# An FFT and GeGLU kernel on one core: value products from two separate matmul passes, sums on DVE, products on POOL, and another split of the PSUM banks

## The chip, the cores and the metric

The kernel runs on one core of one Trainium2 chip. The metric is the device time of one execution in microseconds (us). The engines are PE (TensorE matmuls; its weight loads are listed apart as PEld), DVE (VectorE), ACT (ScalarE), POOL (GpSimd) and SP, whose queue issues nearly all the stores.

## The reference

```python
x = np.fft.fft(np.fft.fft(x, axis=1), axis=2).real        # x: 8 x 3008 x 256
x = x.reshape(24064, 256)
g   = x @ w_gate                                          # 256 -> 1536
val = x @ w_val
out = (0.5 * g * (1 + erf(g / sqrt(2))) * val) @ w_out    # 1536 -> 256
```

## The kernel before

For each of 8 batches the kernel makes the transform with matmuls (stages A, Z and then E and O), and then the feed-forward part. The symmetry of a real input's transform is used: the values of a pair of mirrored tokens are E + O and E - O. A batch is cut into three chunks of 512, 512 and 481 columns, and the 1536 features into 12 blocks of 128, so there are 24 x 12 = 288 blocks. For the gate and for the value, a block accumulates E and O in a PSUM bank, the result for the first token of each pair is read, and then a third matmul with the weights M = -2 x O turns the same bank into the mirrored token's result. That makes six matmuls a block.

```python
def l1_first(ci, fc):                     # per block: E + O
    pg, pv = ps_g(), ps_v()
    for nm, ps in (("g", pg), ("v", pv)):
        nc.tensor.matmul(ps[:, :n], W[nm, "E"][:, fs], EO[:, 0, ...], start=True, stop=False)
        nc.tensor.matmul(ps[:, :n], W[nm, "O"][:, fs], EO[:, 1, ...], start=False, stop=True)
    gl = gelu_tile()
    nc.scalar.activation(gl[:, :n], pg[:, :n], AF.Gelu)
    nc.vector.tensor_tensor(st["h"][:, fc, 0, :n], gl[:, :n], pv[:, :n], op=ALU.mult)

def l1_second(ci, fc):                    # one block later: the mirrored tokens
    for nm, ps in (("g", pg), ("v", pv)):
        nc.tensor.matmul(ps[:, :n], W[nm, "M"][:, fs], EO[:, 1, ...], start=False, stop=True, ...)
    ...                                   # gelu on ACT, product on DVE, written in reverse order
# l2_unit: 12 matmuls h x w_out into ps_o, evicted by ACT, stored from SP
# PSUM, eight banks: gate g 2, value v 2, output o 2, transforms dft 2
```

The transform of the next batch is woven into the blocks of the present one as filler, and a scheduler fixes the order of the instructions on each engine when the kernel is built.

## Time and profile before

The median is 757.7 us (756.9 to 758.0). The first three lines of the profile's page give the span, and for each engine the busy time, its share of the span and the number of instructions:

```profile
span 755.9 us, 14118 instructions
## 1 busy us (share of the span) xinstructions
PE 732.6 (97%) x5328; PEld 478.6 (63%) x5328; DVE 491.7 (65%) x826; ACT 441.4 (58%) x829; POOL 24.2 (3%) x57
...
```

The view by windows shows a stretch of the steady state: its length, then the busy time of PE, PEld, DVE, ACT and POOL with their instruction counts, the clock, and the DMA share and GB/s:

```profile
...
core 0: us, PE busy (x) PEld busy (x) DVE busy (x) ACT busy (x) POOL busy (x), PEclk, DMA share, GB/s
...
350.00:450.00 100.00, 99.70 (x736) 66.04 (x735) 65.67 (x109) 58.89 (x110) 1.02 (x2) 1.00 0.23 50
...
```

In the view of groups (line, engine, operation, tiles, shapes, count, then total busy us, the mean ns of one, and the engine's idle time before them with what ended it), these are the groups that the change touches, and the output matmuls:

```profile
...
L519 PE MATMUL ps_o<-Wo_sb,h_sb 128*128 128x256 bf16 x2112 | 273.1, 272 | 0.5 <-DVE out_sb L530 0.5
...
L484 DVE TENSOR_TENSOR h_sb<-gelu_sb,ps_v 128x512 bf16<-128x512 bf16 x192 | 131.9, 687 | 122.5 <-ACT gelu_sb L483 74.2 <-PE ps_v L481 28.9 <-PE ps_g L496 7.7
L502 DVE TENSOR_TENSOR h_sb<-gelu_sb,ps_v 128x512 bf16<-128x512 bf16 x192 | 130.8, 682 | 28.7 <-ACT gelu_sb L500 27.3
...
L496 PE MATMUL ps_g<-EO_sb,WgM 128*128 128x512 bf16 x192 | 72.9, 380 | 1.1 <-ACT gelu_sb L483 0.7
...
```

The view of waits, for PE alone (us in total, how often, the longest):

```profile
...
PE ps_g L349 <- DVE x_sb L227: 10.6, 4, 5.5
PE ps_o L349 <- DVE x_sb L227: 3.2, 2, 2.3
PE ps_g L496 <- ACT gelu_sb L483: 0.7, 1, 0.7
...
```

PE is busy 99.7 of 100 us, has no idle time worth naming outside the first microseconds, and is the only engine near its limit. A 512-column matmul is recorded as 0.380 us, but consecutive ones start 0.215 us apart. This is the timeline (start, duration in us, engine, what) of a stretch in the middle:

```profile
...
308.02 0.69 DVE L484 TENSOR_TENSOR h_sb<-gelu_sb,ps_v 128x512 bf16<-128x512 bf16 x1 [1.17 <-ACT gelu_sb L483]
308.13 0.38 PE L496 MATMUL ps_v<-EO_sb,WvM 128*128 128x512 bf16 x1
...
308.34 0.38 PE L496 MATMUL ps_g<-EO_sb,WgM 128*128 128x512 bf16 x1
...
308.62 1.01 DVE L365 CAST A_sb<-ps_dft 128x384 bf16<-128x384 f32 x2
308.76 0.38 PE L496 MATMUL ps_v<-EO_sb,WvM 128*128 128x512 bf16 x1
...
```

Between 308.34 and 308.76 PE stood still for 0.2 us, and began again just after the DVE product that reads a value bank (308.02 to 308.71) had ended. No view counts this as idle, because the record of the earlier matmul lasts until 308.72. The Trainium skill says why one must expect it (Perfetto Trace Analysis, section "Tensor Engine Instruction"): the end of a matmul in the profile is estimated from its size, not observed.

### The profile page before, as it was taken

The numbers are of one execution on the slowest core, as the hardware profiler recorded it, in microseconds if no ns is written. First come the engines' busy times: TensorE is split into PE (matmuls) and PEld (weight loads), VectorE is DVE, ScalarE is ACT, GpSimd is POOL, SyncE is SP. The second block draws the span as 40 slices with busy tenths as digits, with TensorE's granted clock in tenths as the row PEclk, the third lists the DMA queues.
The fourth block names the chain that finished last, engine by engine and source line by source line (L and its number), as shares of the span: only waits on it lengthen the run. The fifth ranks groups of instructions, "written<-read, shape, count | busy, mean of one in ns | idle before, by whom it ended". The sixth has DMA issues, their size and how long they took to land.

```text
span 755.9 us, 14118 instructions
## 1 busy us (share of the span) xinstructions
PE 732.6 (97%) x5328; PEld 478.6 (63%) x5328; DVE 491.7 (65%) x826; ACT 441.4 (58%) x829; POOL 24.2 (3%) x57
## 2 busy tenths in 40 slices
PE   2999999999999999999999999999999999999997
PEld 2545666666666666666666666666666666666566
DVE  7688667666676666766667665676666766655552
ACT  5666565556655656556655565656565565655551
POOL 7200000000000000000000000000000000000000
PEclk9999999999999999999999999999999999999999
DMA  9941511421115111151112411111111111111113
GB/s 240 214 86 25 114 29 43 87 64 30 43 32 118 32 39 36 36 111 39 39 34 43 107 39 33 43 29 39 30 43 31 38 29 43 33 39 39 43 40 69
DMA packets 36228, 43.42 MB, mean 57 GB/s; under 512 B 6620, under 2 KB 33244, under 8 KB 34652
## 3 DMA queue, kind: packets, MB, share of 16 engines
q1 hardware_dynamic: 32432, 30.47, 17.0%
q0 software_dynamic: 3136, 11.57, 8.1%
q8 instruction: 41, 0.67, 0.4%
q10 hardware_dynamic: 592, 0.49, 0.3%
q14 instruction: 27, 0.22, 0.1%
HBM read 29.43 MB, written 24.64 MB: 72 GB/s over the span
## 4 chain that ended last, share of the span: by engine, by line
PE 96%; DVE 2%; ACT 1%; issue 1%; DMA 1%; ACTq 0%
PE ps_o L519 33%; PE ps_g L480 9%; PE ps_v L480 9%; PE ps_v L496 9%; PE ps_g L496 8%; PE ps_g L481 8%; PE ps_v L481 8%; PE ps_dft L386 5%; PE ps_dft L349 3%; PE ps_dft L424 1%; PE ps_dft L411 1%; DVE x_sb L227 1%; DMA x_plain<-in_x_dram 1%; ACT gelu_sb L483 0%; PE ps_g L317 0%
## 5 line engine op out<-in xcount | busy, mean ns | idle before, releaser
L484 DVE TENSOR_TENSOR h_sb<-gelu_sb,ps_v 128x512 bf16<-128x512 bf16 (+1 forms) x288 | 195.1, 678 | 193.3 <-ACT gelu_sb L483 116.6
L519 PE MATMUL ps_o<-Wo_sb,h_sb 128*128 128x256 bf16 (+1 forms) x2304 | 298.6, 272 | 0.5 <-DVE out_sb L530 0.5
L519 PEld LDWEIGHTS <-h_sb 128*128 128x128 bf16 (+1 forms) x2304 | 227.2, 100 | 80.1 <-issue 8.6
L483 ACT ACTIVATE gelu_sb<-ps_g 128x512 bf16<-128x512 f32 (+1 forms) x288 | 169.5, 589 | 155.3 <-PE ps_g L481 153.5
L502 DVE TENSOR_TENSOR h_sb<-gelu_sb,ps_v 128x512 bf16<-128x512 bf16 (+1 forms) x288 | 193.2, 671 | 46.6 <-ACT gelu_sb L500 45.2
L500 ACT ACTIVATE gelu_sb<-ps_g 128x512 bf16<-128x512 f32 (+1 forms) x288 | 169.2, 588 | 36.1 <-PE ps_g L496 34.8
L496 PE MATMUL ps_g<-EO_sb,WgM 128*128 128x512 bf16 (+1 forms) x288 | 108.2, 376 | 1.1 <-ACT gelu_sb L483 0.7
L480 PE MATMUL ps_g<-EO_sb,WgE 128*128 128x512 bf16 (+1 forms) x288 | 107.8, 374 | 0.9
L496 PE MATMUL ps_v<-EO_sb,WvM 128*128 128x512 bf16 (+1 forms) x288 | 108.0, 375 | 0.7
L480 PE MATMUL ps_v<-EO_sb,WvE 128*128 128x512 bf16 (+1 forms) x288 | 107.8, 374 | 0.7
L481 PE MATMUL ps_g<-EO_sb,WgO 128*128 128x512 bf16 (+1 forms) x288 | 108.1, 375 | 0.0
L481 PE MATMUL ps_v<-EO_sb,WvO 128*128 128x512 bf16 (+1 forms) x288 | 108.0, 375 | 0.0
L537 ACT ACTIVATE out_sb<-ps_o 128x512 f32<-128x512 f32 x92 | 54.9, 597 | 77.0 <-PE ps_o L519 77.0
L386 PE MATMUL ps_dft<-CS,A_sb 128*128 128x256 bf16 x368 | 57.3, 274 | 0.0
L386 PEld LDWEIGHTS <-A_sb 128*128 128x128 bf16 x384 | 38.3, 100 | 25.7 <-issue 1.5
L349 PEld LDWEIGHTS <-x_sb 94*128 94x128 bf16 x512 | 32.0, 102 | 32.7 <-DVE x_sb L227 14.9
L481 PEld LDWEIGHTS <-WvO 128*128 128x128 bf16 x288 | 28.0, 97 | 31.3 <-issue 8.8
L396 DVE CAST Z_sb<-ps_dft 128x512 bf16<-128x512 f32 x66 | 45.1, 685 | 2.2 <-PE ps_dft L386 2.2
L480 PEld LDWEIGHTS <-WvE 128*128 128x128 bf16 x288 | 28.1, 98 | 26.1 <-issue 1.3
L365 DVE CAST A_sb<-ps_dft 128x384 bf16<-128x384 f32 x84 | 44.5, 551 | 0.1
L481 PEld LDWEIGHTS <-WgO 128*128 128x128 bf16 x288 | 28.0, 97 | 19.1 <-issue 13.2
L496 PEld LDWEIGHTS <-WvM 128*128 128x128 bf16 x288 | 28.1, 98 | 14.8 <-issue 0.7
(96 smaller groups left out, 319.8 us busy)
## 6 DMA issues: line engine op xcount, KB each, us to landing
out_dram<-out_sb SPq DMA_DIRECT2D x361, 64.0 KB, 2.0
x_sb<-in_x_dram POOLq DMA_DIRECT2D x14, 752.0 KB, 10.1
x_plain<-in_x_dram SPq DMA_DIRECT2D x4, 384.0 KB, 7.9
x_plain<-in_x_dram SPq DMA_DIRECT2D x2, 768.0 KB, 8.0
Wo_sb<-in_moe_w_out_dram POOLq DMA_DIRECT2D x2, 384.0 KB, 6.3
wg_hi<-in_moe_w_gate_dram SPq DMA_DIRECT2D x2, 256.0 KB, 3.7
wv_hi<-in_moe_w_val_dram SPq DMA_DIRECT2D x2, 256.0 KB
wg_lo<-in_moe_w_gate_dram SPq DMA_DIRECT2D x2, 256.0 KB, 4.4
```

The source lines that it names most:

```text
L349: nc.tensor.matmul(ps[:, jj * 96 : (jj + 1) * 96], xt[:, j0 + jj, cc * 128 : (cc + 1) * 128], G[:, j0 + jj, :], start=True, stop=True,)
L386: nc.tensor.matmul(ps[:, d * C : (d + 1) * C], A[:, cc, k2 + d, :], CS[:, cc, :], start=(cc == 0), stop=(cc == 1),)
L396: nc.vector.tensor_copy(_sub(Z, [[1, 2 * C]], k2 * C), ps)
L480: nc.tensor.matmul(ps[:, :n], W[nm, "E"][:, fs], EO[:, 0, c0 : c0 + n], start=True, stop=False)
L481: nc.tensor.matmul(ps[:, :n], W[nm, "O"][:, fs], EO[:, 1, c0 : c0 + n], start=False, stop=True)
L483: nc.scalar.activation(gl[:, :n], pg[:, :n], AF.Gelu)
L484: nc.vector.tensor_tensor(st["h"][:, fc, 0, :n], gl[:, :n], pv[:, :n], op=ALU.mult)
L496: nc.tensor.matmul(ps[:, :n], W[nm, "M"][:, fs], EO[:, 1, c0 : c0 + n], start=False, stop=True, skip_group_check=True)
L500: nc.scalar.activation(gl[:, :n], pg[:, :n], AF.Gelu)
L502: nc.vector.tensor_tensor(_sub(st["h"], [[-1, n]], (fc * 2 + 1) * TOK + n - 1), gl[:, :n], pv[:, :n], op=ALU.mult)
L519: nc.tensor.matmul(pso[:m, sign, :], st["h"][:, fc, sign, h0 : h0 + m], Wo_sb[:, fc, :], start=(fc == 0), stop=(fc == NFC - 1),)
L537: nc.scalar.activation(osb[:m], pso[:m], AF.Copy)
```

## The change

PE streams fewer columns. In two blocks in three the value is not accumulated: one matmul leaves E in a value bank, one leaves -2 x O in another, and DVE forms both sums. That drops one of the six matmuls. For this, channel 128, which sits in row 0 of O and which M leaves out, must be added to E by other means: PE broadcasts it once per chunk to all partitions (weights read with stride 0), and DVE adds it times a column of weights. POOL then makes one product for both tokens. To make room, the value gets three banks and the output one; the first transform packs rotate through seven banks instead of eight; the A casts go to ACT, and all later Z casts to DVE. The SBUF tiles for the output get three buffers instead of four, and a gelu tile now holds both tokens.

```diff
+    def apart(ci, fc):
+        return fc % 3 != 2 and (b, ci) != (0, 0)
 # l1_first, in such a block:
+        mm(pv, n, "v", "E", fs, E, True, True)
+        po = ps_v()
+        mm(po, n, "v", "M", fs, O, True, True)
+        nc.vector.scalar_tensor_tensor(ve[:, :n], EB_bufs[b][:, c0 : c0 + n], w128[:, fc : fc + 1],
+                                       pv[:, :n], op0=ALU.mult, op1=ALU.add)
+        nc.vector.scalar_tensor_tensor(vv[:, 0, :n], po[:, :n], -0.5, ve[:, :n], ...)
+        nc.vector.scalar_tensor_tensor(_sub(vv, [[-1, n]], TOK + n - 1), po[:, :n], 0.5, ve[:, :n], ...)
 # l1_second, in such a block: no value matmul, no DVE product
+        nc.gpsimd.tensor_tensor(st["h"][:, fc, :, :n], gl[:, :, :n], pv[:, :, :n], op=ALU.mult)
 # banks
-        ... tag="v", bufs=2 ...      tag="o", bufs=2
+        ... tag="v", bufs=3 ...      tag="o", bufs=1
-            tag = ("dft", "g", "v", "o")[turn[0] % 4]
+            tag, n = (("dft", 2), ("g", 2), ("v", 3))[turn[0] % 3]
 # the O pack: 128 columns (O and channel 128) become 64 + 64
+                    nc.tensor.matmul(ps[:, off : off + n], _sub(st["Z"], [[0, 128]], k2 * C + 128),
+                                     TPI[:, 0:n], start=True, stop=True)      # then cast to EB by ACT
 # evictions
-                s1_ev(j0, "VA" if j0 % 8 == 4 else "VV")
+                s1_ev(j0, "AA")
-                if (k2 // 2) % (2 if b == 0 else 4) == 1:     # Z cast on ACT, else DVE
+                if b == 0 and k2 // 2 % 2 == 1:
 # ... tiles, loads of w128, scratch tiles: cut
```

More of the change, by code (lines that the diff above doesn't have):

```diff
@@ L106, in h_tile, with EB_tile, ve_tile, v_tile @@
         return work_pool.tile([128, NFC, 2, TOK], BF16, tag="h", bufs=2, name="h_sb")
+    def EB_tile():
+        return work_pool.tile([128, HALF], BF16, tag="EB", bufs=2, name="EB_sb")
     def gelu_tile():
-        return work_pool.tile([128, TOK], BF16, tag="gelu", bufs=4, name="gelu_sb")
+        return work_pool.tile([128, 2, TOK], BF16, tag="gelu", bufs=4, name="gelu_sb")
+    def ve_tile():
+        return work_pool.tile([128, TOK], FP32, tag="ve", bufs=2, name="ve_sb")
+    def v_tile():
+        return work_pool.tile([128, 2, TOK], FP32, tag="v", bufs=2, name="v_sb")
     def osb_tile():
-        return work_pool.tile([128, 2, C], FP32, tag="osb", bufs=4, name="out_sb")
+        return work_pool.tile([128, 2, C], FP32, tag="osb", bufs=3, name="out_sb")
     def ps_g():
@@ L117, in ps_v @@
     def ps_v():
-        return psum_pool.tile([128, 512], FP32, tag="v", bufs=2, name="ps_v")
+        return psum_pool.tile([128, 512], FP32, tag="v", bufs=3, name="ps_v")
     def ps_o():
-        return psum_pool.tile([128, 2, C], FP32, tag="o", bufs=2, name="ps_o")
+        return psum_pool.tile([128, 2, C], FP32, tag="o", bufs=1, name="ps_o")
     def ps_dft():
@@ L164 @@
     rd = work_pool.tile([128, 2 * NPH], FP32, tag="Z", bufs=1, name="rd")
-    fp = const_pool.tile([128, C], FP32)
-    rp = const_pool.tile([128, C], FP32)
-    dc = const_pool.tile([128, C], FP32)
+    small = work_pool.tile([128, 4, C], FP32, tag="v", bufs=2, name="small")
+    fp, rp, dc, off = (small[:, i, :] for i in range(4))
     dt_ = const_pool.tile([128, 2 * K1], FP32)
-    off = const_pool.tile([128, C], FP32)
     col_m = const_pool.tile([128, 1], FP32)
@@ L176 @@
     dump = const_pool.tile([1, 1], FP32)
+    w128 = const_pool.tile([128, NFC], FP32)
     w_lo, w_hi = {}, {}
@@ L301, in load_w, with load_w128 @@
                         in_=ap_replace(w, ap=[[F, 128], [1, n]], offset=w.offset + r0 * F + f0))
+    def load_w128():
+        nc.gpsimd.dma_start(
+            out=w128[:, :],
+            in_=ap_replace(moe_w_val, ap=[[1, 128], [128, NFC]], offset=moe_w_val.offset + 128 * F))
     def load_wo():
@@ L325 @@
     EO_bufs = [None] * B
+    EB_bufs = [None] * B
     turn = [0]
@@ L332, in ps_any @@
             turn[0] += 1
-            tag = ("dft", "g", "v", "o")[turn[0] % 4]
-            return psum_pool.tile([128, 512], FP32, tag=tag, bufs=2, name=f"ps_{tag}")
+            tag, n = (("dft", 2), ("g", 2), ("v", 3))[turn[0] % 3]
+            return psum_pool.tile([128, 512], FP32, tag=tag, bufs=n, name=f"ps_{tag}")
         return ps_dft()
@@ L415, in e_pack, with b_pack, run, o_pack @@
             return run
-        def o_pack(gi, half):
+        def b_pack(gi):
+            def run():
+                if "EB" not in st:
+                    st["EB"] = EB_tile()
+                    EB_bufs[b] = st["EB"]
+                ps = st["ps_b"] = ps_dft()
+                for off, k2, n in cols[gi]:
+                    nc.tensor.matmul(
+                        ps[:, off : off + n], _sub(st["Z"], [[0, 128]], k2 * C + 128), TPI[:, 0:n],
+                        start=True, stop=True)
+                n = chunk_len[gi]
+                nc.scalar.activation(_sub(st["EB"], [[1, n]], chunk_off[gi]), ps[:, :n], AF.Copy)
+            return run
+        def o_pack(gi):
             def run():
@@ L420, in run @@
                 ps = ps_dft()
-                part = [c for c in cols[gi] if c[0] // 256 == half]
-                base = half * 256
-                for off, k2, n in part:
+                for off, k2, n in cols[gi]:
                     nc.tensor.matmul(
-                        _sub(ps, [[256, 2], [1, n]], off - base),
-                        st["Z"][:, k2, 128:256], _sub(TPI, [[K1, 2], [1, n]], 0), start=True, stop=True)
-                n = min(256, chunk_len[gi] - base)
-                off = HALF + chunk_off[gi] + base
-                nc.vector.tensor_copy(_sub(EO, [[1, n]], off), ps[:, 256 : 256 + n])
+                        ps[:, off : off + n], st["Z"][:, k2, 128:256], TPI[:, K1 : K1 + n], start=True, stop=True)
+                n = chunk_len[gi]
+                off = HALF + chunk_off[gi]
+                nc.vector.tensor_copy(_sub(EO, [[1, n]], off), ps[:, :n])
                 nc.scalar.activation(
-                    _sub(EO, [[1, n]], off, part_num=1), _sub(ps, [[1, n]], 0, part_num=1), AF.Copy)
+                    _sub(EO, [[1, n]], off, part_num=1), _sub(st["ps_b"], [[1, n]], 0, part_num=1), AF.Copy)
             return run
@@ L439, in dft_work @@
             work.append(e_pack(gi))
-            work.append(o_pack(gi, 0))
-            work.append(o_pack(gi, 1))
+            work.append(b_pack(gi))
+            work.append(o_pack(gi))
         return (work, s1_mm, s1_ev) if b == 0 else work
@@ L466, in ffn_work, with mm @@
         cstate = {}
+        def apart(ci, fc):
+            return fc % 3 != 2 and (b, ci) != (0, 0)
+        def mm(ps, n, nm, part, fs, src, start, stop, **kw):
+            nc.tensor.matmul(ps[:, :n], W[nm, part][:, fs], src, start=start, stop=stop, **kw)
         def l1_first(ci, fc):
             def run():
-                EO = EO_bufs[b]
                 n = chunk_len[ci]
                 c0 = chunk_off[ci]
+                E, O = (EO_bufs[b][:, i, c0 : c0 + n] for i in range(2))
                 if ci not in cstate:
@@ L476, in run @@
                 fs = slice(fc * 128, (fc + 1) * 128)
-                pg, pv = ps_g(), ps_v()
-                st["ps"][fc] = (pg, pv)
-                for nm, ps in (("g", pg), ("v", pv)):
-                    nc.tensor.matmul(ps[:, :n], W[nm, "E"][:, fs], EO[:, 0, c0 : c0 + n], start=True, stop=False)
-                    nc.tensor.matmul(ps[:, :n], W[nm, "O"][:, fs], EO[:, 1, c0 : c0 + n], start=False, stop=True)
-                gl = gelu_tile()
-                nc.scalar.activation(gl[:, :n], pg[:, :n], AF.Gelu)
-                nc.vector.tensor_tensor(st["h"][:, fc, 0, :n], gl[:, :n], pv[:, :n], op=ALU.mult)
+                pg = ps_g()
+                mm(pg, n, "g", "E", fs, E, True, False)
+                mm(pg, n, "g", "O", fs, O, False, True)
+                gl = gelu_tile()
+                nc.scalar.activation(gl[:, 0, :n], pg[:, :n], AF.Gelu)
+                pv = ps_v()
+                if apart(ci, fc):
+                    mm(pv, n, "v", "E", fs, E, True, True)
+                    po = ps_v()
+                    mm(po, n, "v", "M", fs, O, True, True)
+                    ve = ve_tile()
+                    nc.vector.scalar_tensor_tensor(
+                        ve[:, :n], EB_bufs[b][:, c0 : c0 + n], w128[:, fc : fc + 1], pv[:, :n],
+                        op0=ALU.mult, op1=ALU.add)
+                    vv = v_tile()
+                    nc.vector.scalar_tensor_tensor(
+                        vv[:, 0, :n], po[:, :n], -0.5, ve[:, :n], op0=ALU.mult, op1=ALU.add)
+                    nc.vector.scalar_tensor_tensor(
+                        _sub(vv, [[-1, n]], TOK + n - 1), po[:, :n], 0.5, ve[:, :n], op0=ALU.mult, op1=ALU.add)
+                    st["ps"][fc] = (pg, vv, gl)
+                else:
+                    mm(pv, n, "v", "E", fs, E, True, False)
+                    mm(pv, n, "v", "O", fs, O, False, True)
+                    nc.vector.tensor_tensor(st["h"][:, fc, 0, :n], gl[:, 0, :n], pv[:, :n], op=ALU.mult)
+                    st["ps"][fc] = (pg, pv, gl)
             return run
@@ L488, in run @@
             def run():
-                EO = EO_bufs[b]
                 n = chunk_len[ci]
                 c0 = chunk_off[ci]
+                O = EO_bufs[b][:, 1, c0 : c0 + n]
                 st = cstate[ci]
                 fs = slice(fc * 128, (fc + 1) * 128)
-                pg, pv = st["ps"].pop(fc)
-                for nm, ps in (("g", pg), ("v", pv)):
-                    nc.tensor.matmul(
-                        ps[:, :n], W[nm, "M"][:, fs], EO[:, 1, c0 : c0 + n],
-                        start=False, stop=True, skip_group_check=True)
-                gl = gelu_tile()
-                nc.scalar.activation(gl[:, :n], pg[:, :n], AF.Gelu)
-                nc.vector.tensor_tensor(
-                    _sub(st["h"], [[-1, n]], (fc * 2 + 1) * TOK + n - 1), gl[:, :n], pv[:, :n], op=ALU.mult)
+                pg, pv, gl = st["ps"].pop(fc)
+                mm(pg, n, "g", "M", fs, O, False, True, skip_group_check=True)
+                if apart(ci, fc):
+                    nc.scalar.activation(_sub(gl, [[-1, n]], TOK + n - 1), pg[:, :n], AF.Gelu)
+                    nc.gpsimd.tensor_tensor(st["h"][:, fc, :, :n], gl[:, :, :n], pv[:, :, :n], op=ALU.mult)
+                else:
+                    mm(pv, n, "v", "M", fs, O, False, True, skip_group_check=True)
+                    nc.scalar.activation(gl[:, 1, :n], pg[:, :n], AF.Gelu)
+                    nc.vector.tensor_tensor(
+                        _sub(st["h"], [[-1, n]], (fc * 2 + 1) * TOK + n - 1),
+                        gl[:, 1, :n], pv[:, :n], op=ALU.mult)
             return run
@@ L601 @@
         nc.gpsimd.tensor_copy(dump, w_hi["v"][0:1, F - 1 : F])
+        load_w128()
         load_wo()
```

## The prediction

> **What bounds it now.** TensorE. The page has PE busy 732.6 of 755.9 us (97%), the chain that ended last is 96% PE, and in every 100 us stretch from 150 to 650 us PE is busy 99.7 us, while DVE is busy 65 to 66 and ACT 59 to 60. PE's own waits add up to under 17 us, nearly all in the head. Granted clock 1.00. POOL is busy 24 us. One batch takes about 89 us.
>
> **Removed from PE.** A block (128 features x one chunk) has six matmuls of 512 or 481 columns; two blocks in three drop one. In the timeline consecutive 512-column matmuls start 0.215 us apart, so 481 columns cost about 0.203. The first chunk is left out: 15 chunks x 8 x 0.215 + 8 x 8 x 0.203 = 39 us. All of it is on the critical path.
>
> **Added to PE.** The O matmul of 128 columns becomes two of 64, one with channel 128 broadcast as weights: the same columns, 192 more weight loads. The eight 64-column matmuls of the E pack take about 0.24 us in the timeline, 30 ns each, so splitting costs a few ns apiece: 1 to 3 us in all, if a stride-0 weight load is as fast as a dense one. PE floor: 757.7 - 39 + 2 = 721 us.
>
> **DVE** (per batch with DFT work, now 58 us). Two products (0.687, 0.682 us) become three scalar_tensor_tensor in 24 of 36 blocks; that operation took 0.74 to 0.75 us at 128x512 in the weight fold, so I take 0.71 to 0.74: 24 x 2.15 = 51 us, plus 24 products 16, 12 Z casts 8, 3 O casts 2: 78 us. The 12 A casts go to ACT. PE will need about 84 us. By phase it is tighter: where Z and EO are made DVE needs about 2.28 us a block and PE 2.31; where A is made ACT needs 2.16 (two gelus 1.18, A 0.78, output 0.20) and PE 2.26. Both helpers become nearly full, coupled to PE through three value banks and two gate banks.
>
> **POOL.** 184 products of 1024 elements. The trace has 0.61 to 0.94 us for 256 elements; the Trainium skill (GPSIMD Engine Reference, section 3.1) measures 4497 ns for 2048, so 2.1 to 2.4 us by estimate, 4.7 us in the 7 us of three blocks: busy about 430 us, off the critical path. The skill (SBUF, Who interferes with whom) says a DVE instruction with one SBUF input does not contend with POOL; all the new ones have one SBUF and one PSUM tensor. The trace of before can't show this.
>
> **Sum.** Floor 721 plus stalls of some 2% (PE waiting for a value bank that DVE still reads, or for ps_dft and ps_g behind ACT): 735 us.
>
> **What would show it.** PE matmuls down 184 of 512/481 columns and up 192 of 64; PE busy about 715 and 96 to 98% of the span; DVE 600 to 630 us (83%); ACT 480 to 500; POOL 400 to 470. New PE waits: ps_v on the DVE sums, 5 to 20 us in total.
>
> **What would make it wrong.** POOL locking DVE out after all (products over 3 us, or DVE sums over 0.9): then about 760 or more. DVE sums at 0.69 and no stalls: 722. Broadcast weight loads at 100 ns each: +10 us. An instruction order fixed by a schedule that thinks DVE or POOL faster than it is: stalls in every block, 745 to 755.
>
> Chances: faster by over 2% 0.73, within 2% 0.23, slower 0.04. Range 722 to 750.

## The result, and the profile after

The changed kernel took 719.1 us (718.6 to 719.7), a ratio of 0.949 with a 95% interval of 0.948 to 0.951. A ratio here is the mean time of one kernel's fast runs over that of the other's of the same rounds, so it is not quite the ratio of the medians quoted. The direction was as predicted, but the time lies below the stated range (722 to 750): the gain is 38.6 us, where 22.7 were forecast. The same views as before:

```profile
span 716.7 us, 14298 instructions
## 1 busy us (share of the span) xinstructions
PE 688.0 (96%) x5274; PEld 460.5 (64%) x5336; DVE 572.3 (80%) x923; ACT 466.9 (65%) x892; POOL 412.2 (58%) x242
...
```

```profile
...
core 0: us, PE busy (x) PEld busy (x) DVE busy (x) ACT busy (x) POOL busy (x), PEclk, DMA share, GB/s
...
350.00:450.00 100.00, 99.16 (x774) 67.12 (x781) 82.26 (x133) 65.66 (x127) 60.31 (x31) 1.00 0.25 54
...
```

```profile
...
L551 POOL TENSOR_TENSOR h_sb<-gelu_sb,v_sb 128x1024 bf16<-128x1024 bf16 x120 | 257.2, 2144 | 190.2 <-ACT gelu_sb L550 104.0 <-DVE v_sb L530 46.7 <-ACT gelu_sb L517 31.0
...
L524 DVE SCALAR_TENSOR_TENSOR ve_sb<-EB_sb,w_97,ps_v 128x512 f32<-128x512 bf16 x120 | 88.6, 744 | 48.4 <-PE ps_v L502 48.4
L528 DVE SCALAR_TENSOR_TENSOR v_sb<-ps_v,ve_sb 128x512 f32<-128x512 f32 x120 | 82.5, 687 | 8.9 <-POOL h_sb L551 0.5
L530 DVE SCALAR_TENSOR_TENSOR v_sb<-ps_v,ve_sb 128x512 f32<-128x512 f32 x120 | 81.7, 681 | 0.0
...
```

```profile
...
PE ps_g L365 <- DVE x_sb L236: 6.5, 2, 5.5
...
PE ps_v L502 <- DVE v_sb L530: 0.2, 1, 0.2
```

PEld counts 5336 weight loads, 5328 - 184 + 192, as predicted; PE shows only 5274 because this trace lost 62 matmul records. POOL's product takes 2.14 us and POOL is busy 412 us, both within the prediction. DVE is busy 572 us where 600 to 630 were forecast, and in the stretch where Z and EO are made (392 to 454.5 us) it is busy 52.5 of 62.5 us, 84%, where the prediction had it nearly full (2.28 of 2.31 us). ACT, forecast as nearly full where A is made, is busy 17.8 of 22.5 us there, 79%. The timeline shows one part of the reason:

```profile
...
300.10 0.74 DVE L524 SCALAR_TENSOR_TENSOR ve_sb<-EB_sb,w_97,ps_v 128x512 f32<-128x512 bf16 x1
...
300.97 0.69 DVE L528 SCALAR_TENSOR_TENSOR v_sb<-ps_v,ve_sb 128x512 f32<-128x512 f32 x1
...
301.58 0.68 DVE L530 SCALAR_TENSOR_TENSOR v_sb<-ps_v,ve_sb 128x512 f32<-128x512 f32 x1
...
```

The second sum starts 0.61 us before the third although it is recorded as 0.69 us long: DVE's records overlap by about 0.08 us where instructions follow each other. Adding up their durations, as the prediction did, counts that overlap as work: over this trace the durations come to 628 us, the busy time to 572. The first sum and the one that reads its result do not overlap (0.87 us from start to start). The Trainium skill describes this (Perfetto Trace Analysis, section "Optimizing Scalar/DVE Operations"): the recorded latency holds a write acknowledgement that overlaps with the next instruction. The trace agrees in kind.

The view of waits now gives PE 0.2 us of waiting for value banks. So at first sight the answer is simple: the dropped columns are worth 39 us, 38.6 were gained, nothing else happened. The experiments show that this is wrong.

### Counting the waits that no view shows

Within the traces I took the start times of all matmuls. From one to the next I subtracted the columns of the first at 2.4 columns per ns (matmuls of 64, 256 and 512 columns start 0.029, 0.109 and 0.2155 us before the next one where nothing holds it up, so 0.416 ns a column), and called what was left over 20 ns a wait of PE, put down to the engine whose semaphore update came last before it. Between 60 and 690 us of the trace this gives, in us:

| kernel | all | for value banks (DVE) | for gate banks (ACT's gelu) | for transform banks |
|---|---|---|---|---|
| before | 19.9 | 12.1 | 7.6 | 0.3 |
| before, third value bank (e3) | 9.3 | 0.2 | 7.5 | 1.6 |
| before, third gate bank (f1) | 14.9 | 11.3 | 0.2 | 3.4 |
| changed, dropped matmul put back (e1) | 19.8 | 5.8 | 11.9 | 2.1 |
| changed (trace of e4, complete; same until the last chunk) | 19.8 | 7.3 | 10.6 | 1.9 |

The kernel before held 20 us of waiting that its views show as work, and the changed kernel holds as much, but not the same waits. The attribution rests on inferred semaphore events; the experiments test it.

The count can be checked against the spans. Over their whole traces the kernel before, e3, f1 and e1 stream the same columns, 685.9 us at 2.4 columns per ns. The same count gives them 46.5, 36.8, 42.0 and 47.6 us of waits, those of the first and last microseconds included, and their spans are 755.9, 746.9, 752.0 and 757.7 us. What columns and waits leave over is 23.5 to 24.2 us in all four, so the spans differ as the counted waits do, within 0.7 us.

### The profile page after: what moved, and what is told of

It reads as the page before. It is cut to its first block, busy times and chain, and to the rows that moved or that the text cites. A ratio compares the mean times of both kernels' runs of the same rounds, so it can differ in the third digit from the quotient of the medians.

```text
span 716.7 us, 14298 instructions
## 1 busy us (share of the span) xinstructions
PE 688.0 (96%) x5274; PEld 460.5 (64%) x5336; DVE 572.3 (80%) x923; ACT 466.9 (65%) x892; POOL 412.2 (58%) x242
## 3 DMA queue, kind: packets, MB, share of 16 engines
q1 hardware_dynamic: 32432, 30.47, 17.8%
## 4 chain that ended last, share of the span: by engine, by line
PE 88%; ACT 5%; DVE 4%; issue 2%; DMA 1%; POOL 0%; ACTq 0%; DVEq 0%
PE ps_o L573 33%; PE ps_g L502 23%; PE ps_v L502 20%; PE ps_dft L402 6%; PE ps_dft L365 3%; ACT gelu_sb L517 1%; ACT gelu_sb L554 1%; ACT A_sb L379 1%; PE ps_dft L427 1%; PE ps_dft L440 1%; DVE x_sb L236 1%; ACT out_sb L591 1%; DVE EO_sb L456 1%; PE ps_dft L452 1%; DVE h_sb L536 1%
## 5 line engine op out<-in xcount | busy, mean ns | idle before, releaser
L551 POOL TENSOR_TENSOR h_sb<-gelu_sb,v_sb 128x1024 bf16<-128x1024 bf16 (+1 forms) x184 | 387.1, 2105 | 277.2 <-ACT gelu_sb L550 156.8
L573 PE MATMUL ps_o<-Wo_sb,h_sb 128*128 128x256 bf16 (+1 forms) x2304 | 295.5, 272 | 4.0 <-DVE out_sb L584 2.2
L524 DVE SCALAR_TENSOR_TENSOR ve_sb<-EB_sb,w_97,ps_v 128x512 f32<-128x512 bf16 (+1 forms) x184 | 134.1, 733 | 66.2 <-PE ps_v L502 66.0
L528 DVE SCALAR_TENSOR_TENSOR v_sb<-ps_v,ve_sb 128x512 f32<-128x512 f32 (+1 forms) x184 | 124.4, 676 | 13.9 <-POOL h_sb L551 0.5
L530 DVE SCALAR_TENSOR_TENSOR v_sb<-ps_v,ve_sb 128x512 f32<-128x512 f32 (+1 forms) x184 | 123.3, 670 | 0.0
L555 DVE TENSOR_TENSOR h_sb<-gelu_sb,ps_v 128x512 bf16<-128x512 bf16 (+1 forms) x104 | 69.7, 671 | 32.5 <-ACT gelu_sb L554 32.5
L502 PE MATMUL ps_g<-EO_sb,WgO 128*128 128x512 bf16 (+1 forms) x231 | 86.4, 374 | 0.0
L536 DVE TENSOR_TENSOR h_sb<-gelu_sb,ps_v 128x512 bf16<-128x512 bf16 (+1 forms) x104 | 69.9, 673 | 5.2 <-ACT gelu_sb L517 4.0
L412 DVE CAST Z_sb<-ps_dft 128x512 bf16<-128x512 f32 x88 | 60.1, 684 | 1.3 <-PE ps_dft L402 1.3
L402 PE MATMUL ps_dft<-CS,A_sb 128*128 128x256 bf16 x372 | 60.8, 274 | 0.4 <-DVE EO_sb L456 0.3
L365 PEld LDWEIGHTS <-x_sb 94*128 94x128 bf16 x512 | 31.9, 102 | 31.3 <-DVE x_sb L236 14.9
L379 ACT ACTIVATE A_sb<-ps_dft 128x384 bf16<-128x384 f32 x115 | 50.9, 496 | 0.3 <-PE ps_dft L365 0.3
## 6 DMA issues: line engine op xcount, KB each, us to landing
x_sb<-in_x_dram POOLq DMA_DIRECT2D x14, 752.0 KB, 8.1
```

The costliest lines, as they stand in the source:

```text
L402: nc.tensor.matmul(ps[:, d * C : (d + 1) * C], A[:, cc, k2 + d, :], CS[:, cc, :], start=(cc == 0), stop=(cc == 1),)
L502: nc.tensor.matmul(ps[:, :n], W[nm, part][:, fs], src, start=start, stop=stop, **kw)
L524: nc.vector.scalar_tensor_tensor(ve[:, :n], EB_bufs[b][:, c0 : c0 + n], w128[:, fc : fc + 1], pv[:, :n], op0=ALU.mult, op1=ALU.add)
L528: nc.vector.scalar_tensor_tensor(vv[:, 0, :n], po[:, :n], -0.5, ve[:, :n], op0=ALU.mult, op1=ALU.add)
L530: nc.vector.scalar_tensor_tensor(_sub(vv, [[-1, n]], TOK + n - 1), po[:, :n], 0.5, ve[:, :n], op0=ALU.mult, op1=ALU.add)
L536: nc.vector.tensor_tensor(st["h"][:, fc, 0, :n], gl[:, 0, :n], pv[:, :n], op=ALU.mult)
```

## The experiments

Theory A, held when the result was in: PE alone sets the time, nothing ever waited, and the gain is the dropped columns. Rival B: the changed kernel has new waits of 5 to 15 us, as predicted, and something else gave them back.

### e1: put the dropped matmul back as useless work

```diff
                     mm(po, n, "v", "M", fs, O, True, True)
+                    mm(po, n, "v", "M", fs, O, True, True)
```

> The changed kernel with the matmul that it saves put back as useless work: the value's M matmul of each of the 184 blocks is issued twice into the same bank, so TensorE again streams the 39 us of columns, while DVE, ACT and POOL work as in the changed kernel. Theory A (TensorE alone sets the time, there was never any waiting for the helpers, and the gain is exactly the dropped columns): 719.1 + 38.6 = 757.7 us, within 2 us. Rival B (the changed kernel has waits of 5 to 15 us on its helpers, hidden in the total by gains elsewhere): the extra matmuls fill the waits, and the time is 743 to 752 us.

Measured: 760.0 us (759.0 to 760.1), ratio to before 1.003. The extra matmuls were not absorbed by waits: they cost 40.9 us, about what their columns weigh (120 x 0.2155 + 64 x 0.203 = 38.9). And everything in the change except the dropped matmul comes to only +2.3 us against the kernel before. This fits A's number, and refutes B in the form that the extra work would fill the waits. It does not show that there are no waits, only that they stay when PE gets more to do in between.

### e2: the broadcast matmuls twice

```diff
-                for off, k2, n in cols[gi]:          # in the broadcast pack
+                for off, k2, n in cols[gi] * 2:
```

> The changed kernel with every one of the 192 broadcast matmuls of channel 128 (weights read with stride 0, 64 columns) issued twice. If a stride-0 weight load is as fast as a dense one, each costs the 27 to 30 ns of its 64 columns: 5 to 6 us more, 724 to 725 us. If the weight load sets the pace at its recorded 0.10 us: 19 us more, 738 us.

Measured: 725.4 us (725.1 to 725.5), 6.3 us more than the changed kernel, 33 ns for each of 192. A stride-0 weight load does not hold its columns up: in the traces the broadcast matmuls start 29 ns apart, as the 64-column matmuls with dense weights do. Splitting the O pack costs about 192 x (33 - 27) ns = 1 us by this estimate, and 0.4 us by the starts (two of 29 ns in place of one of 56 ns, 192 times): at the low end of the predicted 1 to 3 us, or below it.

### e3: the kernel before with the new bank split alone

```diff
-        ... tag="v", bufs=2 ...      tag="o", bufs=2
+        ... tag="v", bufs=3 ...      tag="o", bufs=1
-            tag = ("dft", "g", "v", "o")[turn[0] % 4]
+            tag, n = (("dft", 2), ("g", 2), ("v", 3))[turn[0] % 3]
```

> The kernel before with only the changed split of the PSUM banks (three value banks, one output bank, and the first packs rotating through 7 banks instead of 8). Theory A says that in steady state the banks cost and gain nothing; the trace of the changed kernel shows its last chunk 3.9 us longer because one output bank makes each unit wait for the eviction of the one before, and the first 48 us 3 us shorter. If both come from the banks: end 4 us longer, head 3 us shorter, 757 to 760 us. If the shorter head comes from the split O pack or the A casts instead: 761 to 762 us.

Measured: 748.9 us (748.7 to 749.5), ratio 0.989 (0.987 to 0.990). Nobody expected this: 8.8 us of the gain need nothing of the change but its PSUM banks. All its matmuls are those of the kernel before, and its PE busy time is 10 us less:

```profile
...
PE 722.4 (97%) x5328; PEld 479.1 (64%) x5328; DVE 490.9 (66%) x826; ACT 443.4 (59%) x829; POOL 24.3 (3%) x57
...
```

Its timeline in a like stretch has the matmuls 0.21 to 0.22 us apart, with the value matmuls moved to where DVE's products (the first two lines) no longer hold them up:

```profile
...
306.11 0.68 DVE L484 TENSOR_TENSOR h_sb<-gelu_sb,ps_v 128x512 bf16<-128x512 bf16 x1
306.70 0.68 DVE L502 TENSOR_TENSOR h_sb<-gelu_sb,ps_v 128x512 bf16<-128x512 bf16 x1
...
307.31 0.38 PE L480 MATMUL ps_v<-EO_sb,WvE 128*128 128x512 bf16 x1
...
307.52 0.38 PE L481 MATMUL ps_v<-EO_sb,WvO 128*128 128x512 bf16 x1
...
307.74 0.38 PE L496 MATMUL ps_g<-EO_sb,WgM 128*128 128x512 bf16 x1
...
307.96 0.38 PE L496 MATMUL ps_v<-EO_sb,WvM 128*128 128x512 bf16 x1
...
```

The count of waits gives the same: those for value banks go from 12.1 to 0.2 us. The bank changes the order of the instructions too, since the scheduler uses it; what the bank does by itself and what the order does that it allows was not separated.

Theory A thus falls. From e3 to e1 only the useful parts of the change are added (two passes, POOL, the broadcast, the casts) at equal streamed columns of the feed-forward part, and the time rises by 11.1 us; the counted waits rise from 9.3 to 19.8. So the new scheme does bring waits, as the prediction feared: 5.6 us for value banks and 4.4 for gate banks. B is right in substance: what gave them back is the third value bank. Its 8.8 us were measured in the kernel before; the new scheme with two value banks was not run.

### f1: the spare bank to the gate instead

```diff
-        ... tag="g", bufs=2 ...      tag="o", bufs=2
+        ... tag="g", bufs=3 ...      tag="o", bufs=1
```

> The kernel before with the bank that the output gives up handed to the gate instead of the value (three gate banks, two value banks, one output bank). Counted from the start times of the matmuls between 60 and 690 us, the kernel before lets TensorE wait 12.1 us for value banks (DVE) and 7.3 us for gate banks (ACT); the run with the third value bank had 0.2 and 7.5 left, and was 8.8 us faster. If these counts are real waits that a bank removes: here the gate waits go to under 1 us, the value waits stay near 12, and the time is 750 to 754 us (757.7 - 7 + 3.9 at the end with one output bank - 2 to 3 in the head). If the gain of the other run came from the head or from a better order of the matmuls alone: 757 to 761 us.

Measured: 753.3 us (752.8 to 753.8), ratio 0.995 (0.993 to 0.996). The counted waits for gate banks vanish, those for value banks stay (11.3), and the time falls within the expected range. So the counts predict what a bank is worth, though not exactly: 3 us of new waits for transform banks came with it.

### e4: the last chunk's output units in banks of their own

```diff
+                if last(ci):
+                    tag, nb = TAIL[subs_of[ci].index(sub) * 2 + sign]   # o, dft x2, v x3, g x2
+                    pso = psum_pool.tile([128, 2, C], FP32, tag=tag, bufs=nb, name=f"ps_{tag}")
```

> The changed kernel, with the eight output units of the very last chunk each in a bank of its own (the banks of the transforms, the value and the gate are free by then). If the single output bank is what makes the end longer: 3.5 to 5.5 us less than the changed kernel, 714 to 715.5 us, with the last chunk's output matmuls running without gaps. If the end is bound by the stores or the evictions: no change, 719.

Measured: 714.5 us (713.5 to 714.6), 4.6 us less than the changed kernel. The chain that ended last (start, us, what) shows what the single output bank had done. In the kernel before, seven units of twelve matmuls ran without a gap:

```profile
...
740.32 9.57 PE ps_o L519 x84
...
```

In the changed kernel every unit waits for the eviction of the one before, about 0.5 us each time:

```profile
...
697.23 1.48 PE ps_o L573 x12
...
698.73 0.43 DVE out_sb L584
...
699.21 1.48 PE ps_o L573 x12
...
700.77 0.39 ACT out_sb L587
...
```

With a bank each they run on again:

```profile
...
697.14 1.42 PE ps_o L577 x12
698.56 2.29 PE ps_dft L577 x21
700.85 3.93 PE ps_v L577 x36
704.78 2.63 PE ps_g L577 x24
...
```

The prediction had left this cost out. In the steady state the single output bank is harmless: between 60 and 690 us the count finds no wait for it in e3 or e4. At the end the units follow each other with nothing in between.

### e5: more fixed cost on DVE, same work

```diff
-                    nc.vector.scalar_tensor_tensor(ve[:, :n], ...)
+                    cut = [n * i // 4 for i in range(5)]
+                    for q0, q1 in zip(cut, cut[1:]):
+                        nc.vector.scalar_tensor_tensor(ve[:, q0:q1], ...)
```

> The changed kernel with the first DVE sum of each of the 184 blocks cut into four instructions: the same work, three more fixed costs. From the trace (0.658 us from start to start at 512 columns, of which 0.533 would be elements[...] by the slope between 481 and 512 columns) each cut adds 0.12 to 0.13 us, 0.37 us a block, 69 us of DVE in all, which takes DVE from 80% to about 88% busy. Theory 'full helpers': DVE still has room, no change beyond 3 us, 719 to 722 us. Theory 'bank held longer': TensorE waits for a value bank that DVE still reads even where DVE has idle time elsewhere, so the hidden waits of TensorE for value banks (7 us in the changed kernel, counted from the start times of the matmuls) grow several times: 730 to 745 us.

Measured: 728.9 us (728.7 to 729.7), 9.8 us more; neither theory's range. DVE is busy 632 us, 87%, and in the middle of the kernel about 90%:

```profile
...
369.00:455.00 86.00, 85.32 (x672) 57.34 (x670) 77.57 (x184) 56.39 (x109) 52.24 (x27) 1.00 0.26 55
...
```

There PE loses little: by the same arithmetic on the start times, the time not spent on columns grows from 5.2 to 5.7 us per 100 us between 300 and 650 us. Nor does PE wait for the value banks, as the second theory has it: between 60 and 690 us the counted waits for them fall from 7.3 to 1.4 us, while those for gate banks rise from 10.6 to 16.2. Why, was not tested.

After 650 us, where there is no next batch to transform and PE has less to do per block, it loses about 6.5 us more than in the changed kernel. Of these, 3.8 us are plain waits of PE for POOL's products; POOL in its turn waits mostly for DVE's sums in this run. Another 1.4 us or so are the clock: from 708.2 to 711.6 us, just after the longest of these waits (2.6 us), the granted clock is 0.50, and the 256-column matmuls start 0.213 us apart instead of 0.109. So in the steady state a DVE at 90% costs PE about 0.5 us in 100, and "full helpers stall PE by 2%" is not a law of this kernel.

### e9: the casts back where they were

```diff
-                s1_ev(j0, "AA")
+                s1_ev(j0, "VA" if j0 % 8 == 4 else "VV")
-                if b == 0 and k2 // 2 % 2 == 1:
+                if (k2 // 2) % (2 if b == 0 else 4) == 1:
```

> The changed kernel with the evictions of A and Z as in the kernel before (most A casts on DVE, a quarter of the Z casts on ACT): DVE about 27 us more, ACT about 29 us less. TensorE's hidden waits in the changed kernel are 10 us for gate banks (released by ACT's second gelu) and 7 us for value banks (released by DVE). If ACT's load makes the gate waits: they shrink, and the value waits grow by about as much, 717 to 723 us. If the move of the casts was needed to keep DVE from holding TensorE up: 725 us or more.

Measured: 717.0 us (716.8 to 717.4), 2.1 us faster than the changed kernel. DVE rises from 80 to 83%, and the counted waits for gate banks (ACT) fall from 10.6 to 9.1 us without more for value banks. Moving the casts to spare DVE was a small loss: ACT, which releases the gate banks, was the one to spare.

### e6 and e7: more blocks in two passes

```diff
-            return fc % 3 != 2 and (b, ci) != (0, 0)
+            return fc % 6 != 5 and (b, ci) != (0, 0)        # e6;  e7: return (b, ci) != (0, 0)
```

> The changed kernel with five blocks in six in two passes instead of two in three, and the last chunk's output units in banks of their own (714.5 us with that alone). 46 more matmuls dropped: 9.8 us of columns. If the helpers still follow: 704 to 706 us. If DVE (46 x 0.7 us more, 84% busy) holds value banks longer: 707 to 712 us.

> As the run with five in six, but every block (of all chunks but the first) in two passes: 92 matmuls fewer than in the changed kernel, 19.6 us of columns. DVE then needs about 640 us of 700 (91%), POOL 276 products of 2.1 us, 590 us (84%). If columns alone decide: 695 us. If DVE's hold on the value banks decides: 703 to 715 us.

Both hold the last-chunk banks of e4, so 714.5 us is what they are compared with. Measured: e6 711.2 us (710.8 to 711.6), e7 712.8 us (712.5 to 713.1). Of 9.8 us of dropped columns e6 kept 3.3, of 19.6 e7 kept 1.7; the rest went into waits (counted between 60 and 680 us: 25.5 and 35.2, against 19.6 in e4). In e7 POOL has become a limit of its own, busy 84%: DVE waits for it to release the sums, and PE for its products:

```profile
...
DVE v_sb L528 <- POOL h_sb L551: 32.6, 68, 0.8
...
PE ps_o L577 <- POOL h_sb L551: 7.3, 16, 1.6
...
```

### f2 and f3: combinations

> The changed kernel with the A and Z casts where the kernel before had them (717.0 us alone, 2.1 less) and the last chunk's output units in banks of their own (714.5 alone, 4.6 less). The two gains lie in different stretches, so they should add: 712.3 us, at most 713.5.

> The same with five blocks in six in two passes (with the changed kernel's casts that gave 711.2 us). If ACT's share of the casts made the waits for gate banks there, 708 to 710 us; if DVE is too full for the A casts with five in six, 712 us or more.

f2 joins the edits of e4 and e9: 711.6 us (711.3 to 712.2), ratio to before 0.940. Its gain on the changed kernel is 7.5 us, where the two alone had 2.1 and 4.6: they add, a little better than expected. f3 is f2 with five blocks in six: 712.0 us (711.5 to 712.6), no better, at the edge of the second case expected (DVE too full). f2 and e6 (711.2) are the best versions found, and their ranges overlap.

### f4: the product on DVE

```diff
-                    nc.gpsimd.tensor_tensor(st["h"][:, fc, :, :n], gl[:, :, :n], pv[:, :, :n], op=ALU.mult)
+                    nc.vector.tensor_tensor(st["h"][:, fc, :, :n], gl[:, :, :n], pv[:, :, :n], op=ALU.mult)
```

> The changed kernel with the product of the two-pass blocks on DVE instead of POOL, one instruction of 1024 elements each. [...]1.2 us, 184 times: 219 us more, DVE 572 + 219 = 790 us: DVE sets the time, 790 to 830 us, slower than the kernel before. If DVE takes the bf16 and fp32 operands from SBUF faster than that, 720 to 760.

Measured: 795.7 us (two runs), ratio 1.051: DVE is busy 96% and sets the time, as expected. (In the last 50 us the granted clock was 0.50 for some 11 us, which may have cost a few us besides.)

```profile
...
L551 DVE TENSOR_TENSOR h_sb<-gelu_sb,v_sb 128x1024 bf16<-128x1024 bf16 x120 | 146.4, 1220 | 0.0
...
```

Without POOL the two passes would cost 38 us rather than save 39. This run also tests what the Trainium skill says (SBUF — State Buffer, section "Who interferes with whom"), that a DVE instruction with at most one SBUF input does not contend with POOL: with POOL idle the second and third sums take 685 and 683 ns at 512 columns, with POOL busy 58% of the time 687 and 681. The trace agrees.

## Why the prediction was wrong

Point by point:

- **The dropped matmuls, 39 us, all on the critical path: right.** e1 measures 40.9 us for putting them back.
- **The split O pack, 1 to 3 us: about right**, 0.4 to 1 us (e2).
- **POOL: right.** 2.14 us a product, 412 us busy, no contention with DVE.
- **DVE 600 to 630 us busy, "nearly full": too high.** It was 572 us, because durations that overlap by 0.08 us were added up. e5 shows that even 90% costs PE only about 0.5 us in 100 in the steady state. ACT (480 to 500 us forecast, 467 measured) and PE (about 715 us forecast, 690 in the complete trace of e4) came out lower too.
- **"Floor 721 plus stalls of some 2% ...: 735 us": this step failed.** The stalls were not the mistake. From e3 to e1 the new scheme cost 11.1 us, of which the counted waits explain 10.5; the prediction had allowed 14. The mistake is the floor. It took all of the 757.7 us, but for the dropped columns, as PE's work, because PE was "busy" 99.7 of 100 us. In truth at least 20 us of it were waits, 12 of them for the two value banks, and the third value bank, which the prediction treated only as something the new scheme needs, takes these away: 8.8 us net in e3, even with the longer end. The sum that the runs show is 757.7 - 8.8 (banks, e3) + 11.1 (the new scheme at equal feed-forward columns, e1) - 40.9 (the dropped matmuls) = 719.1. These terms are differences between runs, so they must add up; what they show is which part of the change holds which part of the time. That the prediction's own case "DVE sums at 0.69 and no stalls: 722" comes near the result is luck: the stalls were there.
- **"New PE waits: ps_v on the DVE sums, 5 to 20 us in total": waits of that size are there, but they are not new.** The start times show 7.3 us, where the kernel before had 12.1 for its value banks; the view of waits, where one would look, shows 0.2.
- **Left out:** the single output bank at the end, 4.6 us lost (e4), and the casts moved to ACT, 2.1 us lost (e9).

Three things stay open. The order of the instructions changes with every edit, so a bank's effect and that of the order it allows were not told apart. The new scheme was not run with two value banks, so what the third is worth there is not known. And the 2.0 us by which e1's extra matmuls cost more than their columns are waits by the count (47.6 us in e1, some 45.5 in the changed kernel, from e4's trace up to 690 us and its own after that), but what makes them was not traced.

## What to carry to other kernels

Before you take an engine's busy time as work, compare the recorded duration of an instruction with the distance between the starts of two that follow each other: where records overlap, a wait shorter than the overlap is counted as busy, and a saturated engine may still be waiting for buffers. When a change brings its own buffers, run the old kernel with those buffers alone first, as here, where the banks alone gave 8.8 us in the old kernel, against 38.6 for the whole change. And when a resource is made scarcer, look at the stretches where nothing else runs in between, above all the end.

## What the Trainium skill lacked or had wrong

- Perfetto Trace Analysis, "Tensor Engine Instruction" and "Identifying the Most-Contended Engine": they say that matmul ends are estimated and that matmul busy time is a bad metric. They don't say that this hides real waits, nor how many: here 20 us of 757.7 in waits of up to 0.2 us each, beside a view of waits that shows almost none of them, since a 512-column matmul is recorded as 0.380 us and the next can start after 0.215. The MFU that the second section advises instead would show how much is not columns, not which waits; the starts less the columns show both.
- The same page's advice that consistent bubbles can mean too few PSUM buffers is right, but the bubbles are not visible as gaps: one more value bank gave 8.8 us where PE showed 99.7% busy.
- Perfetto Trace Analysis, "Optimizing Scalar/DVE Operations", gives about 125 ns of overhead for DVE on PSUM. With one PSUM input, casts started 0.601 us apart at 512 columns and 0.334 at 256, so 1.04 ns a column and about 67 ns besides; products, and sums with an immediate scalar, started 0.595 to 0.607 us apart at 512 columns, much the same. Only the sum with a per-partition scalar comes to 125 ns (0.658 us at 512 columns, 0.258 at 128 in e5). The records of 0.68 to 0.69 us hold some 0.15 us beyond the columns.
- No page that I read says what a per-partition scalar costs against an immediate one: the sum with one (and a bf16 operand) was recorded as 744 ns, those with an immediate (and an fp32 operand) as 681 to 687 ns. The operand's type is hardly the reason: in the kernel before, the weight fold's sum with a per-partition scalar and an fp32 operand is recorded as 746 to 751 ns.
- No page that I read says how fast weights with stride 0 load: the 64-column matmuls with them start 29 ns apart, as those with dense weights in the E pack do, and e2 paid 33 ns for each more.
- GPSIMD Engine Reference, section 3.1, gives fp32 alone, and other types come close to it: its 4497 ns for 2048 fp32 elements is 2.20 ns each; the product of bf16 and fp32 took 2144 ns for 1024, 2.09 ns each.
